# Projecting 27 instead of 28 features a head, feature by feature, beside a zero column in PSUM

## The chip, the cores and the metric

One NeuronCore of a Trainium2 chip runs the whole kernel. The metric is the device time of one execution in microseconds (us); a smaller number is better. The kernel before takes 399.32 us in the median of three runs (398.23 to 400.27).

## The reference, cut to what matters

Two linear attentions with a learned feature map (A and B, each with 16 heads of 28 features, on the same 2048 x 448 input x) are mixed by a gate per row. For each of the two:

```python
pq = einsum("bhsd,hdf->bhsf", q, w_phi)          # 28 features a head
pk = einsum("bhsd,hdf->bhsf", k, w_phi)
phi_q = concatenate([softmax(pq), softmax(-pq)])  # 56 features a head
phi_k = concatenate([softmax(pk), softmax(-pk)])
kv = einsum("bhsf,bhsd->bhfd", phi_k, v);  z = sum over s of phi_k
o = einsum("bhqf,bhfd->bhqd", phi_q, kv) / (einsum("bhqf,bhf->bhq", phi_q, z) + 1e-6)
y = o @ wo                                        # then g * y_A + (1 - g) * y_B
```

A softmax doesn't change when the same number is subtracted from all of its inputs. The two softmaxes of a head therefore need only the differences between its 28 projected features.

## The kernel before, in words

The rows of x are worked in 16 tiles of 128 (index t or k, i). Everything is float32, and products that need it are split into a high and a low part (`wkh`/`wkl`, `wqh`/`wql`, `wvh`/`wvl`, `xg`). The instructions are issued in the order in which the program is written, engine by engine; each engine works strictly in that order, and waits between engines come from which tile an instruction reads or writes. The order is therefore the schedule. In the profile PE is the matrix engine, PEld its weight loads, DVE, ACT and POOL the vector, scalar and GpSimd engines, SP the queue that issues all the DMAs.

**Start.** The projection weights of K are folded with `w_phi` on the chip: `bd` (L114) is a block-diagonal copy of `w_phi`, four heads in a block, and `fold` (L116 to L125) multiplies each 128-row part of the K weights by it: eight matmuls of 112 columns into a PSUM tile, a copy of the result to the high part on ACT (L124), the rest to the low part on DVE (L125). Ahead of the four folds 16 transposes of an identity run on PE into the same pool of PSUM tiles (`pw`, L244). In the trace each of these fp32 products is two PE records, so that 64 records stand for four folds.

**K and V phase** (loop at L264, 16 steps). A step of PE is the K projection (`proj`, L127 to L138: 11 matmuls for A, 11 for B, 448 columns each, into one PSUM tile of two banks), the V projection (the same with 450 and 448 columns) and `kv_acc` of the step before (L185, into the PSUM tile `one`). `shift` (L143) then reads the K tile four times on DVE: maximum (L147), minimum (L148), x minus the maximum (L151), the minimum minus x (L152), 896 elements a partition each; ACT takes exponentials (L154), DVE the sums (L161) and a reciprocal (L162), POOL multiplies (L165). The steps 2 to 5 also fold one part of the Q weights each. The pool `two` hands its three PSUM tiles of two banks out in turn to `pw`, the folds and all the projections.

**Q front.** `q_front` (L193) reads a Q projection from PSUM three times on DVE: a maximum over the features (L198, 896 elements) and the subtraction for A and for B (L200, 448 elements each), into `uq`. Four DMAs write that to DRAM (`qd`, L205) and one reads it back in another layout (`tq`, L206). Later `q_exp0`, `q_min`, `q_exp1` and `q_turn` (L212, L216, L217, L221, L229) take `tq` to the transposed features. The Q tiles 0 to 3 are projected in the last K and V steps (t = 13, 14) and right behind them (L316, L321), in that order with the turns of the tiles 0 and 1.

**Between the phases.** SP issues, behind the DMAs of the Q tiles, two large reads of the output weights (L325) and then the gate's small ones (`gates`, L253: L258 and L260); POOL and DVE need the gate for the first output tile (L261, L368 to L376).

**Output phase** (loop at L419). Step i: PE runs `num(i)` (L352), the Q projection i + 4 into its only PSUM tile `q` (L417), and the output matmul of tile i - 2 (L408). DVE runs, in this order, the transposition of `num` (`n_turn`, L358), a reciprocal (L367), the minimum of Q tile i + 2 (L216), two transpositions of o (L388, L389), a reciprocal (L374), `q_front(i + 4)` (L198, L200), L397 and `q_turn(i + 2)` (L229). The Q work ends with i = 11. In the last two tiles DVE also runs what POOL runs otherwise (L368 to L382); the gate is read there with a step of 16 elements (L375, `gate[:, None, :, :, i]`), and column DH of `ctrs` with a step of 32 (L368).

Of the kernel before, what the change touches and what calls it, by code (L numbers as in the profile page):

```python
# [8 lines left out]
F32 = mybir.dt.float32  # L9
F32R = mybir.dt.float32r  # L10
AF = mybir.ActivationFunctionType
OP = mybir.AluOpType
AX = mybir.AxisListType

P = 128
S, D, H, DH = 2048, 448, 16, 28
# [3 lines left out]
NP = H // 2  # L20
PF = 4 * DH
VC = 2 * D + 2
HP = 32
WARM = 16
LEAD = 4
# [5 lines left out]
def hedgehog_mix(ctx: ExitStack, tc: tile.TileContext, xd, wv, wkt, wqt, wphi, wo, cmask, cpmask, out):  # L31
    nc = tc.nc
# [3 lines left out]
    one_stack = ExitStack()  # L36
    one = one_stack.enter_context(tc.tile_pool(name="one", bufs=1, space=bass.MemoryType.PSUM))
    two_stack = ExitStack()
    two = two_stack.enter_context(tc.tile_pool(name="two", bufs=3, space=bass.MemoryType.PSUM))


    xg = [const.tile([P, 7, GT], F32R, name=f"xg{g}") for g in range(NG)]
# [1 line left out]
    gate = const.tile([P, 2, 4, NT], F32, name="gate")  # L44
    kvs = const.tile([P, 2, 2, 4, HP], F32, name="kvs")
    kvt = const.tile([P, 2, 2, 4, HP], F32, name="kvt")
    work = ctx.enter_context(tc.tile_pool(name="work", bufs=2))
# [7 lines left out]
    wp_ = ctx.enter_context(tc.tile_pool(name="wts", bufs=1))  # L55
# [5 lines left out]
    raw = start.enter_context(tc.tile_pool(name="raw", bufs=1, side="right"))  # L61
    ident = raw.tile([P, P], F32, name="ident")
    make_identity(nc, ident)
    mask = raw.tile([PF, 4], F32, name="mask")
    wp = raw.tile([PF, 2, 4, HP], F32, name="wp")
    bd = wp_.tile([PF, 2, 4, PF], F32, name="bd")
    wkh = wp_.tile([P, 4, 2 * D], F32R, name="wkh")
    wkl = wp_.tile([P, 4, 2 * D], F32R, name="wkl")
    wvh = wp_.tile([P, 4, VC], F32R, name="wvh")
    wvl = wp_.tile([P, 4, VC], F32R, name="wvl")  # L70
    NV = 2
# [24 lines left out]
    def load_wv(c):  # L96
        wvr[c] = raw.tile([P, VC], F32, name=f"wvr{c}")
        nc.sync.dma_start(wvr[c], wv[c * P:(c + 1) * P, :])
# [7 lines left out]
    wt = load_wt(wkt, 128)  # L106
# [3 lines left out]
    load_x(0, P, 2 * P, GT)  # L110
    for v in vs:
        nc.gpsimd.memset(v[:, :, :, :, DH:], 1.0)
    for q in range(4):
        nc.vector.tensor_scalar(bd[:, :, :, q * DH:(q + 1) * DH], wp[:, :, :, :DH], mask[:, q:q + 1], None, op0=OP.mult)  # L114

    def fold(c, wt, wh, wl):  # L116
        ps = two.tile([P, 2, 512], F32, name="two")
        for b in range(2):
            for g in range(4):
                nc.tensor.matmul(ps[:, b, g * PF:(g + 1) * PF], wt[:, b, g, c * P:(c + 1) * P], bd[:, b, g],  # L120
                                 start=True, stop=True)
        dh = wh[:, c, :].rearrange("p (b f) -> p b f", b=2)
        dl = wl[:, c, :].rearrange("p (b f) -> p b f", b=2)
        nc.scalar.activation(dh, ps[:, :, :D], AF.Copy)  # L124
        nc.vector.tensor_tensor(dl, ps[:, :, :D], dh.bitcast(F32), OP.subtract)  # L125

    def proj(t, wh, wl, widths, ps):  # L127
        x = xg[t // 4]
        o = (t % 4) * P
        lo = 0  # L130
        for b, n in enumerate(widths):
            terms = [(c, wh, c) for c in range(3)] + [(4 + c, wh, c) for c in range(3)]
            terms += [(3, wh, 3)] + [(c, wl, c) for c in range(4)]
            for i, (xc, w, wc) in enumerate(terms):
                nc.tensor.matmul(ps[:, b, :n], x[:, xc, o:o + P], w[:, wc, lo:lo + n],  # L135
                                 start=i == 0, stop=i == len(terms) - 1)
            lo += n
        return ps  # L138

    def hb(ap):  # L140
        return ap.rearrange("p b (h f) -> p b h f", f=DH)

    def shift(ps):  # L143
        p4 = hb(ps[:, :, :D])
        mx = ph.tile([P, 2, 2, H], F32, name="mx")
        e = ph.tile([P, 2, HA * DH], F32, name="e")
        nc.vector.tensor_reduce(mx[:, 0], p4, AX.X, OP.max)  # L147
        nc.vector.tensor_reduce(mx[:, 1], p4, AX.X, OP.min)  # L148
        e5 = e.rearrange("p s (b h f) -> p s b h f", b=2, f=DH)
        bc = [mx[:, s, :, :, None].to_broadcast([P, 2, H, DH]) for s in range(2)]  # L150
        nc.vector.tensor_tensor(e5[:, 0], p4, bc[0], OP.subtract)  # L151
        nc.vector.tensor_tensor(e5[:, 1], bc[1], p4, OP.subtract)  # L152
        for s in range(2):
            nc.scalar.activation(e[:, s], e[:, s], AF.Exp)  # L154
        return e
# [37 lines left out]
    def q_front(k, ps):  # L193
        seq[k] = len(seq) % 2
        u = uqs[k % len(uqs)]
        mx = work.tile([P, 2, H], F32, name="qmx")
        p4 = hb(ps[:, :, :D])
        nc.vector.tensor_reduce(mx, p4, AX.X, OP.max)  # L198
        for b in range(2):
            nc.vector.tensor_tensor(u[:, :, b], p4[:, b].rearrange("p (r g) f -> p r g f", r=4),  # L200
                                    mx[:, b].rearrange("p (r g) -> p r g", r=4)[:, :, :, None].to_broadcast([P, 4, 4, DH]),
                                    OP.subtract)
        m = qd[seq[k]]
        for c in range(4):
            nc.sync.dma_start(m[:, :, c].rearrange("r t x -> t r x"), u[32 * c:32 * c + 32].rearrange("p r b g f -> p r (b g f)"))  # L205
        nc.sync.dma_start(tq[seq[k]].rearrange("p c b g f -> p (c b g f)"), m.rearrange("r t c x -> (r t) (c x)"))  # L206
# [26 lines left out]
    def split_wo(c):  # L233
        n = 3 * D * (c % 2)
        st = [wtb[:, n + D * i:n + D * i + D] for i in range(3)]
        nc.sync.dma_start(st[0], wos[:, HP * c:HP * (c + 1), :])
        split_w(st[0], st[1].bitcast(F32R), st[2].bitcast(F32R), nc.gpsimd)
# [1 line left out]
            nc.sync.dma_start(wod[i][:, c], st[1 + i])  # L239


    pw = two.tile([P, 2, 512], F32, name="two")
    for i in range(WARM):
        nc.tensor.transpose(pw[:, 0, :P], ident, ident)  # L244
    for c in range(4):
        fold(c, wt, wkh, wkl)
        if c == 1:
            split_x(0, 0, P, nc.gpsimd)

    def two_tile():  # L250
        return two.tile([P, 2, 512], F32, name="two")

    def gates(lo, hi):  # L253
        gl = glog[:, lo:hi]
# [7 lines left out]

    phi = {}
    for t in range(NT):  # L264
        pk = proj(t, wkh, wkl, (D, D), two_tile())
        if t == 0:
            for c in range(4):
                split_w(wvr[c], wvh[:, c, :], wvl[:, c, :], nc.vector if c < 3 else nc.gpsimd)
            split_x(0, P, 2 * P, nc.gpsimd)
            split_x(0, 2 * P, GT, nc.gpsimd)  # L270
            load_x(1, 0, GT)
            wt = load_wt(wqt, 512)
            w5 = wos.rearrange("g (r b f) n -> b g r (f n)", r=4, b=2)
            for b in range(2):
                nc.sync.dma_start(w5[b], wo[b * D:(b + 1) * D, :].rearrange("(r g f) n -> g r (f n)", r=4, g=4))
        e = shift(pk)
        n = t - T0 - 1
        if 0 <= n < 2:
            q_exp0(n)
            q_min(n)  # L280
            q_exp1(n)
        phi[t] = k_soft(e)
        v_out(t, proj(t, wvh, wvl, (D + 2, D), two_tile()))
        if t in (1, 3, 5):
            g = (t + 1) // 2
            split_x(g, 0, GT, nc.gpsimd)
            if g + 1 < NG:
                load_x(g + 1, 0, GT)
        if t == 0:

            start.close()
            qp = ctx.enter_context(tc.tile_pool(name="qp", bufs=1, side="right"))
            wqh = qp.tile([P, 4, 2 * D], F32R, name="wqh")
            wql = qp.tile([P, 4, 2 * D], F32R, name="wql")
            uqs = [qp.tile([P, 4, 2, 4, DH], F32, name="uq")]
            tq = [qp.tile([P, 4, 2, 4, DH], F32, name=f"tq{i}") for i in range(2)]
        if 2 <= t < 6:
            fold(t - 2, wt, wqh, wql)
        if t == 6:
            eq = xrb.rearrange("p (s a c f) -> p s a c f", s=2, a=8, c=4)  # L300
            nc.gpsimd.memset(eq[:, :, :, :, DH:], 0.0)
            nc.gpsimd.memset(kvs, 0.0)
        if t > 0:
            kv_acc(t - 1, phi.pop(t - 1))
        if 6 <= t < 13:
            split_wo(t - 6)
        if t == NT - 4:
            gates(0, t + 1)
        if 0 <= n < 2:
            q_turn(n)  # L310
        n = t - T0
        if 0 <= n < 2:
            q_front(n, proj(n, wqh, wql, (D, D), two_tile()))


    q_front(2, proj(2, wqh, wql, (D, D), two_tile()))  # L316
    cb = [wp_.tile([P, 3592], F32, name=n) for n in ("wvh", "wvl")]
    ctrs = [c[:, :2048].rearrange("p (r b s c m) -> p r b s c m", r=4, b=2, s=2, m=HP) for c in cb]
    oTs = [c[:, 2048:2048 + (7 - MID) * P].rearrange("p (k t) -> p k t", t=P) for c in cb]
    uqs.append(cb[0][:, 2560:2560 + 2 * D].rearrange("p (r b g f) -> p r b g f", r=4, b=2, g=4))  # L320
    q_front(3, proj(3, wqh, wql, (D, D), two_tile()))  # L321
    woh = wp_.tile([P, 7, D], F32R, name="wkh")
    wol = wp_.tile([P, 7, D], F32R, name="wkl")
    for w, d in ((woh, wod[0]), (wol, wod[1])):
# [15 lines left out]
    qps = ctx.enter_context(tc.tile_pool(name="qps", bufs=1, space=bass.MemoryType.PSUM))  # L340
# [73 lines left out]
        nc.sync.dma_start(out[i * P:(i + 1) * P, :], ob)  # L414

    def q_proj(k):
        return proj(k, wqh, wql, (D, D), qps.tile([P, 2, 512], F32, name="q"))  # L417

    for i in range(NT + 2):  # L419
        f, m = i + LEAD, i + 2  # L420
        if i == 0:
            pq = q_proj(f)
        if i < NT:
            ps = num(i)
# [67 lines left out]
```

## Time and profile before

| | |
|---|---|
| median of three runs | 399.32 us (398.23 to 400.27) |
| span of the profiled execution, first to last instruction | 396.4 us |
| what lies around the span, against the median | 2.9 us |
| start (identity transposes, folds of K), to the first K matmul | 0 to 15 us |
| K and V phase | 15 to 161 us |
| Q tiles 0 to 3, with the last two K and V steps | 161 to 201 us |
| between the phases | 201 to 238 us |
| output phase with Q projections | 238 to 346 us |
| output phase without them | 346 to 396 us |

The profiled execution has no time of its own beside its span; the 2.9 us are the difference to the median. A row of a timeline reads: start, duration, engine, line, operation, output <- inputs, shape, and in brackets the idle time of the engine before it with what ended it. A row of the groups reads: count, total busy time, mean nanoseconds of one, idle time before.

### The profile page before, as it was taken

How to read it: one execution, taken by the hardware profiler on the slowest of the kernel's cores; microseconds unless marked ns; L12 is line 12 of the kernel's file. 1: busy time of each engine (PE TensorE's matmuls, PEld its weight loads, DVE VectorE, ACT ScalarE, POOL GpSimd, SP SyncE). 2: the span in 40 equal slices, each digit the busy share in tenths (PEclk: the TensorE clock that was granted, in tenths of full speed). 3: DMA queues.
4: the chain of work that ended last, by engine and by line, in shares of the span. 5: the costliest groups of instructions: out<-in, count | busy, mean ns of one | idle time of the engine just before them, and what ended most of it. 6: DMA issues, size and time to landing. Idle time of an engine off the chain costs nothing.

```text
span 396.4 us, 10423 instructions
## 1 busy us (share of the span) xinstructions
PE 360.8 (91%) x4608; PEld 320.3 (81%) x4608; DVE 294.0 (74%) x321; ACT 122.8 (31%) x174; POOL 220.6 (56%) x182
## 2 busy tenths in 40 slices
PE   8999999999999999999983089999999999997765
PEld 8999999999999999889872078988888888875544
DVE  1676767666666667669743299999999999988991
ACT  2744353233333333221400033333223333332112
POOL 0184816375444444304400299999888898889311
PEclk9999999999999999999997579999999999999989
DMA  7928411100222222131158133434443324420001
GB/s 179 311 65 268 182 48 56 53 25 25 88 68 67 67 67 70 28 95 46 48 132 319 64 94 94 117 119 118 117 119 115 102 69 120 116 96 26 25 23 46
DMA packets 27218, 38.52 MB, mean 97 GB/s; under 512 B 3733, under 2 KB 21893, under 8 KB 26885
## 3 DMA queue, kind: packets, MB, share of 16 engines
q1 hardware_dynamic: 27172, 37.85, 31.7%
q8 instruction: 36, 0.59, 0.6%
q14 instruction: 10, 0.07, 0.1%
HBM read 23.62 MB, written 15.84 MB: 100 GB/s over the span
## 4 chain that ended last, share of the span: by engine, by line
PE 71%; DMA 9%; DVE 9%; POOL 4%; SPq 3%; issue 2%; ACT 1%; POOLq 0%; DVEq 0%; ACTq 0%
PE two L135 33%; PE out L408 14%; PE q L135 12%; PE num L352 5%; PE two L120 4%; PE one L185 3%; DMA gd<-glog 3%; DMA qd<-uq 2%; DMA tq<-qd 2%; SPq L205 2%; POOL xrb L217 2%; DVE qmx L198 1%; DVE uq L200 1%; DVE wvh L358 1%; DMA wtb<-in_wkt 1%
## 5 line engine op out<-in xcount | busy, mean ns | idle before, releaser
L165 POOL TENSOR_TENSOR e<-e,rs 128x896 f32<-128x896 f32 x32 | 53.8, 1703 | 66.1 <-DVE rs L162 66.1
L408 PE MATMUL out<-wkh,e 128*128 128x448 f32 x224 | 52.8, 373 | 10.9 <-ACT bd L413 6.5
L154 ACT ACTIVATE e<-e 128x896 f32<-128x896 f32 x32 | 30.2, 954 | 98.7 <-DVE e L151 98.6
L135 PE MATMUL q<-wqh,xg 128*128 128x448 f32 x168 | 40.9, 384 | 17.3 <-DVE uq L200 14.5
L408 PEld LDWEIGHTS out<-wkh,e 128*128 128x128 f32 x224 | 41.5, 189 | 17.5 <-ACT bd L413 8.0
L135 PE MATMUL two<-wkh,xg 128*128 128x448 f32 x224 | 51.8, 369 | 0.0
L135 PE MATMUL two<-wvh,xg 128*128 128x450 f32 (+1 forms) x224 | 50.9, 366 | 0.0
L135 PEld LDWEIGHTS q<-wqh,xg 128*128 128x128 f32 x168 | 31.7, 194 | 22.6 <-DVE uq L200 14.9
L147 DVE TENSOR_REDUCE mx<-two 128x32 f32<-128x896 f32 x16 | 17.5, 1091 | 39.4 <-PE two L135 39.4
L135 PEld LDWEIGHTS two<-wvh,xg 128*128 128x128 f32 x224 | 42.1, 188 | 3.4
L135 PEld LDWEIGHTS two<-wkh,xg 128*128 128x128 f32 x224 | 40.9, 188 | 4.0 <-POOL xg L87 0.4
L217 POOL TENSOR_TENSOR xrb<-qmn,tq 128x896 f32<-128x896 f32 x16 | 28.2, 1762 | 23.7 <-DVE qmn L216 19.9
L229 DVE STREAM_TRANSPOSE wtb<-xrb 128x2048 f32<-128x2048 f32 x16 | 36.9, 2304 | 3.1 <-ACT xrb L221 3.1
L161 DVE TENSOR_REDUCE sm<-e 128x32 f32<-128x896 f32 x32 | 33.3, 1081 | 1.1
L352 PE MATMUL num<-wtb,kvt 32*32 32x128 f32 x2048 | 31.1, 283 | 2.4 <-DVE wvh L358 2.4
L352 PEld LDWEIGHTS num<-wtb,kvt 32*32 32x32 f32 x2048 | 25.0, 104 | 9.0 <-issue 3.4
L391 ACT ACTIVATE e<-turn 128x512 fp32r<-128x512 f32 x16 | 9.6, 598 | 70.7 <-DVE turn L388 70.7
L135 PE MATMUL two<-wvl,xg 128*128 128x450 f32 (+1 forms) x128 | 31.2, 365 | 0.0
L135 PE MATMUL two<-wkl,xg 128*128 128x448 f32 x128 | 30.9, 363 | 0.0
L408 PE MATMUL out<-wkl,e 128*128 128x448 f32 x112 | 26.8, 380 | 0.0
L135 PEld LDWEIGHTS two<-wvl,xg 128*128 128x128 f32 x128 | 24.1, 188 | 2.3 <-POOL wvl L102 0.3
L135 PEld LDWEIGHTS two<-wkl,xg 128*128 128x128 f32 x128 | 24.0, 187 | 1.8 <-DVE wkl L125 0.2
(92 smaller groups left out, 623.5 us busy)
## 6 DMA issues: line engine op xcount, KB each, us to landing
tq<-qd SPq DMA_DIRECT2D x16, 448.0 KB
qd<-uq SPq DMA_DIRECT2D x36, 112.0 KB
out<-bd SPq DMA_DIRECT2D x16, 224.0 KB
wod<-wtb SPq DMA_DIRECT2D x14, 224.0 KB
qd<-wvh SPq DMA_DIRECT2D x28, 112.0 KB
xrb<-in_xt SPq DMA_DIRECT2D x3, 1024.0 KB
wvr<-in_wv SPq DMA_DIRECT2D x4, 449.0 KB
wtb<-in_wkt SPq DMA_DIRECT2D x8, 224.0 KB
```

The costliest lines, as they stand in the source:

```text
L120: nc.tensor.matmul(ps[:, b, g * PF:(g + 1) * PF], wt[:, b, g, c * P:(c + 1) * P], bd[:, b, g], start=True, stop=True)
L135: nc.tensor.matmul(ps[:, b, :n], x[:, xc, o:o + P], w[:, wc, lo:lo + n], start=i == 0, stop=i == len(terms) - 1)
L147: nc.vector.tensor_reduce(mx[:, 0], p4, AX.X, OP.max)
L154: nc.scalar.activation(e[:, s], e[:, s], AF.Exp)
L161: nc.vector.tensor_reduce(sm[:, s], e[:, s].rearrange("p (h f) -> p h f", f=DH), AX.X, OP.add)
L165: nc.gpsimd.tensor_tensor(e3, e3, rs[:, s, :, None].to_broadcast([P, HA, DH]), OP.mult)
L185: nc.tensor.matmul(kvp[32 * r:32 * r + DH + 1, b, g], v[:, b, h // 2, h % 2], phi[:, :, hs:hs + DH], start=(t == 0 and b == 0 and g == 0), ...
L217: nc.gpsimd.tensor_tensor(eq[:, 1, :, :, :DH], mn.rearrange("p c a -> p a c")[:, :, :, None].to_broadcast([P, 8, 4, DH]), tview(k), OP.sub ...
L229: nc.vector.transpose(e_slot(k), eq.rearrange("p s a c f -> p (s a c f)"))
L352: nc.tensor.matmul(ps[32 * g:32 * g + 32, r, 2 * b + s], kvt[32 * r:32 * r + 32, b, s, g], eTs[i][32 * r:32 * r + 32, s, b, g], start=True ...
L391: nc.scalar.activation(hl[:, 0, :MID], ps, AF.Copy)
L408: nc.tensor.matmul(ps[:, :D], a, w, start=n == 0, stop=n == len(terms) - 1)
```

## The change

For each head the last column of `w_phi` is subtracted from the other 27 before the folding, so that the 28th feature is zero and isn't projected. `bd` has blocks of 27 columns; a fold's matmuls have 108 columns and its result is read with the features outermost, so that the folded weights are stored feature by feature (27 x 16 heads), 432 columns for A and for B. The K and Q projections write these 432 columns to columns 48 to 479 of a PSUM bank. The columns 480 to 495 are set to zero once, and nothing writes to them again; V keeps its columns 0 to 449. `shift` and `q_front` read columns 48 to 495 as 28 x 16, with the feature innermost: an element step of 16. For the zeros to last, the three PSUM tiles are allocated once and handed out by a counter, and the `q` tile of the output phase is allocated once as well.

```diff
+FD = DH - 1
+FW = H * FD
+FO, FZ = 48, 48 + H * FD
...
+    wpd = raw.tile([PF, 2, 4, FD], F32, name="wpd")
+    bd = wp_.tile([PF, 2, 4, 4 * FD], F32, name="bd")
...
+    nc.vector.tensor_tensor(wpd, wp[:, :, :, :FD], wp[:, :, :, FD:DH].to_broadcast([PF, 2, 4, FD]), OP.subtract)
     for q in range(4):
-        nc.vector.tensor_scalar(bd[:, :, :, q * DH:(q + 1) * DH], wp[:, :, :, :DH], mask[:, q:q + 1], None, op0=OP.mult)
+        nc.vector.tensor_scalar(bd[:, :, :, q * FD:(q + 1) * FD], wpd, mask[:, q:q + 1], None, op0=OP.mult)
+    twos = [two.tile([P, 2, 512], F32, name=f"two{i}") for i in range(3)]
...
+        return twos[turn_of[0] % 3]
...
+    for ps in twos:
+        nc.vector.memset(ps[:, :, FZ:FZ + H], 0.0)
...
     def fold(c, wt, wh, wl):
...
-        dh = wh[:, c, :].rearrange("p (b f) -> p b f", b=2)
-        nc.scalar.activation(dh, ps[:, :, :D], AF.Copy)
-        nc.vector.tensor_tensor(dl, ps[:, :, :D], dh.bitcast(F32), OP.subtract)
+        dh = wh[:, c, :].rearrange("p (b f h) -> p b f h", b=2, f=FD)
+        src = ps[:, :, :FW].rearrange("p b (h f) -> p b f h", f=FD)
+        nc.scalar.activation(dh, src, AF.Copy)
+        nc.vector.tensor_tensor(dl, src, dh.bitcast(F32), OP.subtract)
...
-                nc.tensor.matmul(ps[:, b, :n], x[:, xc, o:o + P], w[:, wc, lo:lo + n],
+                nc.tensor.matmul(ps[:, b, at:at + n], x[:, xc, o:o + P], w[:, wc, lo:lo + n],
...
+    def fm(ps):
+        return ps[:, :, FO:FO + D].rearrange("p b (f h) -> p b h f", h=H)
...
     def shift(ps):
-        p4 = hb(ps[:, :, :D])
+        p4 = fm(ps)
...
-    pw = two.tile([P, 2, 512], F32, name="two")
+    pw = two_tile()
...
-        pk = proj(t, wkh, wkl, (D, D), two_tile())
+        pk = proj(t, wkh, wkl, (FW, FW), two_tile(), FO)
...
     def q_proj(k):
-        return proj(k, wqh, wql, (D, D), qps.tile([P, 2, 512], F32, name="q"))
+        return proj(k, wqh, wql, (FW, FW), qt, FO)
+
+    qt = qps.tile([P, 2, 512], F32, name="q")
+    nc.vector.memset(qt[:, :, FZ:FZ + H], 0.0)
```

`q_front` changes as `shift` does, and the Q weights and the four Q projections outside the output phase as those of K.

More of the change, by code (lines that the diff above doesn't have):

```diff
@@ L38, in hedgehog_mix @@
     two_stack = ExitStack()
-    two = two_stack.enter_context(tc.tile_pool(name="two", bufs=3, space=bass.MemoryType.PSUM))
+    two = two_stack.enter_context(tc.tile_pool(name="two", bufs=1, space=bass.MemoryType.PSUM))
     xg = [const.tile([P, 7, GT], F32R, name=f"xg{g}") for g in range(NG)]
@@ L65, in hedgehog_mix @@
     wp = raw.tile([PF, 2, 4, HP], F32, name="wp")
-    bd = wp_.tile([PF, 2, 4, PF], F32, name="bd")
-    wkh = wp_.tile([P, 4, 2 * D], F32R, name="wkh")
-    wkl = wp_.tile([P, 4, 2 * D], F32R, name="wkl")
+    wpd = raw.tile([PF, 2, 4, FD], F32, name="wpd")
+    bd = wp_.tile([PF, 2, 4, 4 * FD], F32, name="bd")
+    wkh = wp_.tile([P, 4, 2 * FW], F32R, name="wkh")
+    wkl = wp_.tile([P, 4, 2 * FW], F32R, name="wkl")
     wvh = wp_.tile([P, 4, VC], F32R, name="wvh")
@@ L112, in hedgehog_mix, with two_tile, proj @@
         nc.gpsimd.memset(v[:, :, :, :, DH:], 1.0)
+    nc.vector.tensor_tensor(wpd, wp[:, :, :, :FD], wp[:, :, :, FD:DH].to_broadcast([PF, 2, 4, FD]), OP.subtract)
     for q in range(4):
-        nc.vector.tensor_scalar(bd[:, :, :, q * DH:(q + 1) * DH], wp[:, :, :, :DH], mask[:, q:q + 1], None, op0=OP.mult)
+        nc.vector.tensor_scalar(bd[:, :, :, q * FD:(q + 1) * FD], wpd, mask[:, q:q + 1], None, op0=OP.mult)
+    twos = [two.tile([P, 2, 512], F32, name=f"two{i}") for i in range(3)]
+    turn_of = [0]
+    def two_tile():
+        turn_of[0] += 1
+        return twos[turn_of[0] % 3]
+    for ps in twos:
+        nc.vector.memset(ps[:, :, FZ:FZ + H], 0.0)
     def fold(c, wt, wh, wl):
-        ps = two.tile([P, 2, 512], F32, name="two")
+        ps = two_tile()
         for b in range(2):
             for g in range(4):
-                nc.tensor.matmul(ps[:, b, g * PF:(g + 1) * PF], wt[:, b, g, c * P:(c + 1) * P], bd[:, b, g],
+                nc.tensor.matmul(ps[:, b, g * 4 * FD:(g + 1) * 4 * FD], wt[:, b, g, c * P:(c + 1) * P], bd[:, b, g],
                                  start=True, stop=True)
-        dh = wh[:, c, :].rearrange("p (b f) -> p b f", b=2)
-        dl = wl[:, c, :].rearrange("p (b f) -> p b f", b=2)
-        nc.scalar.activation(dh, ps[:, :, :D], AF.Copy)
-        nc.vector.tensor_tensor(dl, ps[:, :, :D], dh.bitcast(F32), OP.subtract)
-    def proj(t, wh, wl, widths, ps):
+        dh = wh[:, c, :].rearrange("p (b f h) -> p b f h", b=2, f=FD)
+        dl = wl[:, c, :].rearrange("p (b f h) -> p b f h", b=2, f=FD)
+        src = ps[:, :, :FW].rearrange("p b (h f) -> p b f h", f=FD)
+        nc.scalar.activation(dh, src, AF.Copy)
+        nc.vector.tensor_tensor(dl, src, dh.bitcast(F32), OP.subtract)
+    def proj(t, wh, wl, widths, ps, at=0):
         x = xg[t // 4]
@@ L196, in q_front @@
         mx = work.tile([P, 2, H], F32, name="qmx")
-        p4 = hb(ps[:, :, :D])
+        p4 = fm(ps)
         nc.vector.tensor_reduce(mx, p4, AX.X, OP.max)
@@ L248, in hedgehog_mix @@
             split_x(0, 0, P, nc.gpsimd)
-    def two_tile():
-        return two.tile([P, 2, 512], F32, name="two")
     def gates(lo, hi):
@@ L292, in hedgehog_mix @@
             qp = ctx.enter_context(tc.tile_pool(name="qp", bufs=1, side="right"))
-            wqh = qp.tile([P, 4, 2 * D], F32R, name="wqh")
-            wql = qp.tile([P, 4, 2 * D], F32R, name="wql")
+            wqh = qp.tile([P, 4, 2 * FW], F32R, name="wqh")
+            wql = qp.tile([P, 4, 2 * FW], F32R, name="wql")
             uqs = [qp.tile([P, 4, 2, 4, DH], F32, name="uq")]
@@ L312, in hedgehog_mix @@
         if 0 <= n < 2:
-            q_front(n, proj(n, wqh, wql, (D, D), two_tile()))
-    q_front(2, proj(2, wqh, wql, (D, D), two_tile()))
+            q_front(n, proj(n, wqh, wql, (FW, FW), two_tile(), FO))
+    q_front(2, proj(2, wqh, wql, (FW, FW), two_tile(), FO))
     cb = [wp_.tile([P, 3592], F32, name=n) for n in ("wvh", "wvl")]
@@ L320, in hedgehog_mix @@
     uqs.append(cb[0][:, 2560:2560 + 2 * D].rearrange("p (r b g f) -> p r b g f", r=4, b=2, g=4))
-    q_front(3, proj(3, wqh, wql, (D, D), two_tile()))
+    q_front(3, proj(3, wqh, wql, (FW, FW), two_tile(), FO))
     woh = wp_.tile([P, 7, D], F32R, name="wkh")
```

## The prediction

> **What bounds the kernel now.** I read the windows by stage first, since one average over the kernel would hide that its stages have different limits. Columns: stretch, its length, then busy time of PE, PEld, DVE, ACT and POOL with their instructions, granted clock, DMA share, GB/s.
>
> ```profile
> 92.00:161.00 69.00, 69.00 (x716) 62.20 (x718) 46.80 (x51) 22.23 (x36) 32.02 (x23) 1.00 0.21 68
> 161.00:201.00 40.00, 39.89 (x425) 35.88 (x412) 29.68 (x31) 10.61 (x16) 13.83 (x9) 1.00 0.19 49
> 201.00:238.00 37.00, 17.63 (x428) 14.84 (x428) 17.70 (x23) 5.46 (x9) 12.39 (x16) 0.72 0.50 162
> 238.00:346.00 108.00, 107.77 (x1652) 94.51 (x1654) 102.67 (x113) 34.50 (x50) 94.76 (x82) 1.00 0.40 110
> ```
>
> PE is never idle in the K and V phase, where DVE has a third to spare. Between the phases nobody is full. In the output phase PE is full again, and DVE nearly so. Next the chain of work that ended last, for what the time hangs on in each stage:
>
> ```profile
> 5.16 10.03 PE two L120 x64
> ...
> 141.67 9.09 PE two L135 x44
> 150.75 0.92 PE one L185 x64
> 151.68 9.09 PE two L135 x44
> ...
> 166.45 1.10 DVE qmx L198
> 167.57 1.17 DVE uq L200 x2
> ...
> 210.79 11.13 DMA gd<-glog
> ...
> 227.24 1.17 DVE uq L200 x2
> ...
> 249.14 4.71 PE q L135 x22
> ```
>
> PE carries it up to the first Q tile, in steps of 151.68 - 141.67 = 10.01 us. From 166 us on it goes through the Q front: DVE work, DMAs, the transposition, then the next Q tile on DVE; at 210.79 the gate's DMA, which SP issues behind the Q tiles, and after it the Q front of tile 4. From 238 us on it is PE. Last, DVE's timeline, for the slack that its readers have: once in the K phase, then its first and last transpositions of `num` in the output phase.
>
> ```profile
> 146.32 1.09 DVE L147 TENSOR_REDUCE mx<-two 128x32 f32<-128x896 f32 x1 [3.17 <-PE two L135]
> ```
>
> ```profile
> 230.83 2.27 DVE L358 STREAM_TRANSPOSE wvl<-num 128x2048 f32<-128x2048 f32 x1
> ...
> 240.82 2.27 DVE L358 STREAM_TRANSPOSE wvh<-num 128x2048 f32<-128x2048 f32 x1
> ...
> 347.04 2.32 DVE L358 STREAM_TRANSPOSE wvh<-num 128x2048 f32<-128x2048 f32 x1 [0.76 <-PE num L352]
> ```
>
> DVE idles 3.17 us of each K and V step. In the output phase its own step, back to back, is 240.82 - 230.83 = 9.99 us; the 11 steps to 347.04 take 116.21 us, 10.6 each, because PE slows the later ones and leaves DVE only 0.76 us a step.
>
> **The change part by part.**
>
> *Shorter projections, the gain.* A K and V step's 44 matmuls take 9.09 us, 206.6 ns each. In proportion 16 columns of 448 would be 7.4 ns. If the weight loads set the spacing it would be nothing: in the folds they seem to, as the next rows show (PE alone: the 16 transposes of 128 columns, and the folds' matmuls of 112 columns early and late).
>
> ```profile
> 1.30:5.10 3.80, 3.68 (x16) 3.28 (x16) 1.00 0.67 173
> ```
>
> ```profile
> 5.10:10.60 5.50, 5.44 (x25) 5.47 (x26) 1.00 1.12 231
> 10.70:15.00 4.30, 4.30 (x40) 4.30 (x39) 1.00 1.10 343
> ```
>
> 128 columns take 0.22 us and 112 columns the same 0.22 us, so that 108 instead of 112 in the folds is worth nothing. (Later the folds take 0.107 each; the granted clock reads 1.00 in both stretches, so it doesn't explain that.) From 112 columns at 107.5 ns to 448 at 206.6 the slope is 0.29 ns a column, 4.7 ns for 16. Between 4.7 and 7.4 I take 6 ns, and keep 0 as an end: 22 x 6 = 0.13 us a projection. On the path lie K0 to K13 and Q0, 15 x 0.13 = 1.95 us, and ten projections of the output phase, 1.3 us. K14, K15 and Q1 to Q3 lie beside the Q front's chain and bring nothing. In all 3.25 us, and only while PE stays the bound.
>
> *Strided reads on DVE, the cost.* Every reader of a projection now steps 16 elements, 64 bytes, from one element to the next. No row of before shows DVE reading PSUM that way. The nearest rows read SBUF: DVE's small products in the last tiles.
>
> ```profile
> L376 DVE TENSOR_TENSOR cdd<-crs,cden 128x64 f32<-128x64 f32 x2 | 0.5, 226 | 0.1
> L375 DVE TENSOR_TENSOR cden<-cden,gate 128x32 f32<-128x32 f32 x2 | 0.4, 214 | 0.1
> L369 DVE TENSOR_TENSOR cden<-cdd 128x32 f32<-128x32 f32 x2 | 0.4, 192 | 0.1
> L368 DVE TENSOR_TENSOR cdd<-wvl,crs 128x64 f32<-128x64 f32 x1 | 0.3, 261 | 0.0
> ```
>
> L375 reads the gate with the very step of 16. Against L369, 32 elements as well, it takes 22 ns more, 0.69 ns an element; L368, with a step of 32, takes 35 ns more than L376 for 64 elements, 0.55. Without stride an element costs (226 - 192) / 32 = 1.06. I bound the price in PSUM by 0 (a different memory) and 1.06 (an element costs two), and take 0.69, the row with the same step.
>
> [...]
>
> Per K step DVE gets 4 x 896 x 0.69 = 2.47 us more. The 3.17 us of idle time hide it, less the 0.13 that PE gives up: 0.57 left. That cover ends at (3.17 + 0.13) / 3584 = 0.92 ns an element. The K tile is held 2.5 us longer. Its next writer is V of the next step, which starts when that step's K is done, a step of 10.01 us after these readers began; four reads of 1.09 + 0.62 are over after 6.9, so this holds nothing up. Per Q tile it is 1792 x 0.69 = 1.24 us, and those lie on the path:
> - Q0, Q1, Q2 and Q4 stand in the chain one behind another (Q3's readers run beside SP's DMAs of Q2): 4 x 1.24 = 4.96 us.
> - In the output phase the step of DVE becomes 9.99 + 1.24 = 11.23, above PE's. Its 11 steps from tile 1 to tile 12 take 123.5 instead of 116.2: +7.3 us. PE's 1.3 us are then worth nothing, since PE waits.
>
> *Start.* The subtraction for `wpd` and four zeroings are added on DVE. The rows there (PE's transposes, DVE behind the mask, K0's waits for x and for the last fold's low part):
>
> ```profile
> 1.34 3.68 PE L244 MATMUL two<-ident 128*128 128x128 f32 x16 [1.34 <-POOL ident masks.py:199]
> ...
> 3.08 1.08 DVE L114 TENSOR_SCALAR bd<-wp,mask 112x224 f32<-112x224 f32 x4 [3.08 <-DMA mask<-in_cmask]
> 4.26 0.48 DVE L175 MEMSET one<- 128x512 f32 x1
> ...
> 15.82 0.71 PEld L135 LDWEIGHTS two<-wkh,xg 128*128 128x128 f32 x4 [0.38 <-POOL xg L87]
> ...
> 17.32 0.19 PEld L135 LDWEIGHTS two<-wkl,xg 128*128 128x128 f32 x1 [0.20 <-DVE wkl L125]
> ```
>
> The zeroing of a PSUM tile stands ahead of the transposes in the program, in the same bank though in other columns, and behind `wpd` and `bd` on DVE. If the transposes wait for it, they start at 3.08 + 0.38 (`wpd`, 216 elements at 1.06 on top of L369's 32) + 1.08 + 0.2 (two zeroings of 32 elements, by L369's 192 ns at most each, overlapping) = 4.75 instead of 1.34. Queued behind them on PE are all the folds, and behind these K0. 16 slots of 0.215 us, as in the rows above, end at 8.2, where the folds start now at 5.16, behind the landing of their weights: +3.05 us on the path. If no wait is set it is 0. If the quick spacing of the folds still sets in at 10.6 us, it is less, about 1.6. The trace can't say which; I take 3.05.
>
> [...]
>
> The last fold's copy (L124) and subtraction (L125) read 896 strided elements each, one after the other: 2 x 896 x 0.69 = 1.24 us. K0 waits for L125 at 17.32 already, so that this is on the path. If ACT reads strides freely, half of it goes. The other zeroing, of the `q` tile, stands behind the gate's small DVE work, and the first Q projection of the output phase waits for it; what that costs ends in the time in which DVE stands still for the gate:
>
> ```profile
> 225.91 0.35 DVE L374 RECIPROCAL cden<-cden 128x32 f32<-128x32 f32 x1 [13.00 <-POOL cden L369]
> ```
>
> That is 13 us of cover.
>
> *Sum.* 3.05 + 1.24 - 1.95 + 4.96 + 7.3 = +14.6 us: a span of 411.0 instead of 396.4, and with the 2.9 us between span and median **413.9 us**.
>
> **The rivals.**
>
> *A: strides in PSUM are free, the transposes wait.* 3.05 less the 0.38 us that K0 now waits for x anyway, - 1.95 - 1.3 = -0.6: **398.7 us**. For it: PSUM isn't SBUF, and the strided rows above are all SBUF.
>
> *B: strides free and no wait, the other side.* -3.25: **396.1 us**, faster. The mechanism is PE's shorter matmul in the two stages where PE is full. It decides where a strided element costs less than 3.25 us / (1792 in the last fold + 4 x 1792 in the Q front) = 0.36 ns more, and in the output phase below (0.76 + 0.13) / 1.792 = 0.50. Against it: L375 and L368 lie above both.
>
> *C: an element costs two, 1.06 more.* The K step's readers need 3.8 us, over the 3.3 there are: DVE's step is 10.01 - 3.17 + 3.8 = 10.64, with a fold's 896 elements at 2.12 it is 12.5, and DVE replaces PE as the bound of the K phase. K0's readers start 5 us late (3.05 and 2 x 896 x 1.06); nine steps and four with a fold bring K13's some 15 us late; K14's and K15's readers then push the Q front's chain, four times 1.9 us come on top, tile 1 of the output phase is some 25 us late, and 11 steps of 11.9 add 14.6: **439 us**. Against it: no row of DVE shows such a price.
>
> *D: the matmuls don't get shorter,* because the loads set their spacing. That takes 3.25 from the gains of A and B (402, 399.3), 1.95 from the forecast's. Against it: the spacing of the 448 is far above the folds' 0.107, whose weights have as many columns. I count it within the others' margins.
>
> **How the numbers follow.** Forecast 0.42, A 0.30, B 0.10, C (or dearer) 0.18. The forecast's own range is 408 (price 0.55, start 1.6) to 420 (price up to 0.9, where the K phase would join). The range of 395.5 to 422 takes in the forecast, A and B, and leaves C out. This kernel's measurement can tell some 0.5% from no change, 2 us. Faster by more: B's 0.10, and 0.08 of A's 0.30 (a wait shorter than 3.05); within: 0.20 of A; slower: 0.42 + 0.18, and 0.02 of A, 0.62.
>
> **What would show it.** L147 to L152 and L198 at about 1.08 + 0.62 = 1.7 us instead of 1.08, and L200 at 0.93 instead of 0.62, would confirm the price; at 1.08, A or B holds; at 2.0, C. The first identity transpose near 4.7 us shows the wait. In the K phase PE must still be back to back, a step about 0.13 us shorter. In the output phase L358 must start every 11.2 us without waiting for `num`, and PE must wait for L200. I am wrong most of all if PSUM serves single elements as fast as runs, for then 13.5 of the 14.6 us go.

## The result and the profile after

The changed kernel takes 394.54 us in the median of six runs (393.09 to 395.19), the kernel before 398.42 us (398.06 to 400.27) beside it. The ratio is 0.9884, with a 95% interval of 0.9863 to 0.9904: 1.2% faster, 3.9 us, where 413.9 us were forecast, 14.6 us more than before. The profiled execution of the changed kernel took 395.19 us, with a span of 393.4.

I begin with the disputed rows, DVE's readers of the projections. These are the groups of the changed kernel on DVE, different shapes kept apart (count, busy time, mean ns of one, idle time before):

```profile
L165 DVE TENSOR_REDUCE mx<-two 128x32 f32<-128x896 f32 x16 | 17.5, 1091 | 38.2 <-PE two L150 38.2
L169 DVE TENSOR_TENSOR e<-two,mx 128x896 f32<-128x896 f32 x16 | 17.3, 1081 | 0.0
...
L216 DVE TENSOR_REDUCE qmx<-q 128x32 f32<-128x896 f32 x12 | 12.3, 1029 | 0.0
...
L218 DVE TENSOR_TENSOR uq<-q,qmx 128x448 f32<-128x448 f32 x12 | 6.9, 620 | 0.2
...
L140 DVE TENSOR_TENSOR wkl<-two,wkh 128x864 fp32r<-128x864 f32 x4 | 4.2, 1058 | 7.9 <-ACT wkh L139 7.9
```

The same groups of the kernel before:

```profile
L147 DVE TENSOR_REDUCE mx<-two 128x32 f32<-128x896 f32 x16 | 17.5, 1091 | 39.4 <-PE two L135 39.4
L151 DVE TENSOR_TENSOR e<-two,mx 128x896 f32<-128x896 f32 x16 | 17.3, 1081 | 0.0
...
L198 DVE TENSOR_REDUCE qmx<-q 128x32 f32<-128x896 f32 x12 | 12.3, 1027 | 0.0
...
L200 DVE TENSOR_TENSOR uq<-q,qmx 128x448 f32<-128x448 f32 x12 | 6.9, 619 | 0.2
```

A step of 16 elements in PSUM costs DVE nothing: 1091 against 1091 ns, 1081 against 1081, 1029 against 1027, 620 against 619. The subtraction of a fold (L140), which now steps 27 elements, takes 1058 ns for 864 elements and took 1092 for 896.

Next the start. The timeline of the changed kernel (start, duration, engine, line, in brackets the idle time before):

```profile
4.25 0.16 DVE L128 MEMSET two<- 128x32 f32 x3
...
4.51 3.37 PE L262 MATMUL two<-ident 128*128 128x128 f32 x16 [4.51 <-DVE two L128]
...
7.72 7.29 PE L134 MATMUL two<-bd,wtb 112*128 112x108 f32 x64
...
14.79 1.74 PE L150 MATMUL two<-wkh,xg 128*128 128x432 f32 x7
...
15.48 0.70 PEld L150 LDWEIGHTS two<-wkh,xg 128*128 128x128 f32 x4 [0.23 <-POOL xg L91]
```

The wait is there, as forecast: the transposes start at 4.51 us (4.75 was estimated, 1.34 was before), released by the zeroing L128. The folds start at 7.72 instead of 5.16. But they now take 7.29 us instead of 10.03, with 64 records both times, and the first K matmul comes at 14.79; the kernel before has it at

```profile
14.96 1.94 PE L135 MATMUL two<-wkh,xg 128*128 128x448 f32 x7
```

so that the forecast's +3.05 us is -0.17 here. K0's fourth product then waits for POOL's part of x, at 15.48 us; in the kernel before it did so at 15.82.

Now the chain of work that ended last, of the changed kernel (start, us, what), in the places that the prediction showed of before:

```profile
140.41 8.99 PE two L150 x44
...
150.32 9.01 PE two L150 x44
...
164.83 1.10 DVE qmx L216
...
208.19 11.61 DMA gd<-glog
...
236.13 6.15 PE q L150 x22
...
248.37 4.54 PE q L150 x22
252.91 4.26 PE out L423 x21
...
259.00 4.54 PE q L150 x22
```

A K step is 150.32 - 140.41 = 9.91 us (10.01 before), and Q0's maximum comes at 164.83 instead of 166.45, 1.62 us earlier. A step of the output phase is 259.00 - 248.37 = 10.63 us. Before, the same chain reads

```profile
249.14 4.71 PE q L135 x22
253.86 4.33 PE out L408 x21
...
260.02 4.71 PE q L135 x22
```

10.88 us; the Q projection gives 0.17 of the difference and, although nothing about it was changed, the output matmul 0.07. The first Q projection of the phase takes 6.15 us instead of 4.54. The windows of the changed kernel show why (stretch, length, PE busy with its instructions, granted clock, DMA share, GB/s):

```profile
236.00:240.00 4.00, 3.87 (x12) 0.57 0.46 115
240.00:246.00 6.00, 6.00 (x32) 1.00 0.22 76
```

The granted clock is 0.57 there and 1.00 behind it. The change doesn't force that: in another execution of the same kernel (e11 below) the same projection takes 4.60 us. Last, DVE's transpositions of `num` in the output phase of the changed kernel:

```profile
228.82 2.27 DVE L373 STREAM_TRANSPOSE wvl<-num 128x2048 f32<-128x2048 f32 x1
...
238.81 2.27 DVE L373 STREAM_TRANSPOSE wvh<-num 128x2048 f32<-128x2048 f32 x1
...
344.10 2.32 DVE L373 STREAM_TRANSPOSE wvh<-num 128x2048 f32<-128x2048 f32 x1 [0.52 <-PE num L367]
```

DVE's own step is 238.81 - 228.82 = 9.99 us as before, and it still waits for PE, 0.52 us a step instead of 0.76. PE is still the bound of this phase.

Where the 3.0 us of the two spans (396.4 - 393.4) went: 1.62 up to Q0's maximum; 0.39 more up to tile 1's transposition (228.82 against 230.83), a stretch in which the gate's DMA takes 11.61 instead of 11.13 us; 116.21 - 115.28 = 0.93 in the 11 steps, of which the low clock has taken some 1.6 back (6.15 - 4.54); behind these nothing (49.3 against 49.4).

### The profile page after: what moved, and what is told of

The parts are those of the page before. It is cut to its first block, busy times and chain, and to the rows that moved or that the text cites. A ratio compares the mean times of both kernels' runs of the same rounds, so it can differ in the third digit from the quotient of the medians.

```text
span 393.4 us, 10387 instructions
## 1 busy us (share of the span) xinstructions
PE 355.6 (90%) x4608; PEld 320.0 (81%) x4608; DVE 294.4 (75%) x326; ACT 122.8 (31%) x174; POOL 220.7 (56%) x182
## 4 chain that ended last, share of the span: by engine, by line
PE 71%; DVE 10%; DMA 8%; POOL 4%; issue 2%; SPq 2%; ACT 2%; POOLq 0%; DVEq 0%; ACTq 0%
PE two L150 33%; PE out L423 14%; PE q L150 12%; PE num L367 5%; PE two L134 4%; PE one L203 3%; DMA gd<-glog 3%; POOL xrb L235 2%; DMA tq<-qd 2%; DMA qd<-uq 2%; DVE wtb L247 1%; SPq L223 1%; DVE wvh L373 1%; DVE wvl L373 1%; DVE qmx L216 1%
## 5 line engine op out<-in xcount | busy, mean ns | idle before, releaser
L150 PE MATMUL q<-wqh,xg 128*128 128x432 f32 x168 | 41.6, 391 | 13.9 <-DVE uq L218 8.9
L150 PE MATMUL two<-wkh,xg 128*128 128x432 f32 x224 | 50.7, 365 | 0.0
L150 PEld LDWEIGHTS q<-wqh,xg 128*128 128x128 f32 x168 | 33.3, 204 | 18.2 <-DVE uq L218 9.4
L165 DVE TENSOR_REDUCE mx<-two 128x32 f32<-128x896 f32 x16 | 17.5, 1091 | 38.2 <-PE two L150 38.2
L150 PE MATMUL two<-wkl,xg 128*128 128x432 f32 x128 | 30.6, 360 | 0.0
L373 DVE STREAM_TRANSPOSE wvh<-num 128x2048 f32<-128x2048 f32 x8 | 18.4, 2306 | 10.4 <-PE num L367 10.4
```

The costliest lines, as they stand in the source:

```text
L150: nc.tensor.matmul(ps[:, b, at:at + n], x[:, xc, o:o + P], w[:, wc, lo:lo + n], start=i == 0, stop=i == len(terms) - 1)
L373: nc.vector.transpose(cb[i % 2][:, :2048], ps.rearrange("p r a t -> p (r a t)"))
```

## The experiments

The theory after the result: strided reads in PSUM are free, the wait of the transposes is covered, and PE's shorter matmuls are the whole gain. Rivals: the strided reads do cost, and something else pays for them; or the zeroing and the fixed tiles bring or take something; or the wait costs what was forecast and hides a larger gain.

**e1: the strided reads alone**, in the kernel before.

```diff
+    def fm(ps):
+        return ps[:, :, :D].rearrange("p b (f h) -> p b h f", h=H)
...
     def shift(ps):
-        p4 = hb(ps[:, :, :D])
+        p4 = fm(ps)
...
-        p4 = hb(ps[:, :, :D])
+        p4 = fm(ps)
         nc.vector.tensor_reduce(mx, p4, AX.X, OP.max)
```

> The kernel before, in which the K and Q readers on DVE take the 448 projected columns of PSUM with a step of 16 elements (so features of different heads are mixed in one softmax; nothing else changes). Theory: a strided element of PSUM costs DVE nothing more, so the maximum over 896 elements stays at 1.09 us, the subtraction of 448 at 0.62, and the time at 398.4 us, within 0.3%. Rival, the price of the prediction (0.69 ns an element): 1.7 and 0.93 us, and about 410.5 us (12 us more: 5 in the Q front, 7.3 in the output phase). Rival, strides free in the changed kernel only because 16 columns lie in a row across heads: not told apart by this run, since the step is the same.

Measured: 399.43 us, ratio 1.0004 [0.9989, 1.0020] to the kernel before. Its groups on DVE:

```profile
L150 DVE TENSOR_REDUCE mx<-two 128x32 f32<-128x896 f32 x16 | 17.5, 1092 | 39.7 <-PE two L135 39.7
...
L201 DVE TENSOR_REDUCE qmx<-q 128x32 f32<-128x896 f32 x12 | 12.3, 1028 | 0.0
...
L203 DVE TENSOR_TENSOR uq<-q,qmx 128x448 f32<-128x448 f32 x12 | 6.9, 620 | 0.2
```

The strided reads are free by themselves, row by row and in the whole time. The first rival falls.

**e2: the shorter matmuls alone.** In each K and Q projection the first of 11 products keeps its 448 columns, the other ten have 432.

```diff
+                m = n - cut if i else n
-                nc.tensor.matmul(ps[:, b, :n], x[:, xc, o:o + P], w[:, wc, lo:lo + n],
+                nc.tensor.matmul(ps[:, b, :m], x[:, xc, o:o + P], w[:, wc, lo:lo + m],
```

> The kernel before, in which 10 of the 11 matmuls of each K and Q product run over 432 instead of 448 columns (the last 16 columns get only the first product; no stride, no new tiles, no zeroing, same start). Theory: all of the gain is PE's shorter matmuls, so that 10/11 of it comes: a K step 9.92 us instead of 10.01, an output step 10.65 instead of 10.87, 394.9 us (-3.5). Rival: part of the gain is the start or the tiles that are allocated once; then this run stays over 396.5 us.

Measured: 395.23 us, ratio 0.9905 [0.9881, 0.9929]. The gain is 0.95%; 11/10 of that is 1.05%, and the whole change gives 1.16%, within the intervals. The chain of e2's profile has the changed kernel's steps as well:

```profile
141.01 9.00 PE two L136 x44
...
150.93 8.98 PE two L136 x44
...
247.47 4.58 PE q L136 x22
...
258.14 4.57 PE q L136 x22
```

A K step is 9.92 us and an output step 10.67, where 9.92 and 10.65 were expected. So PE's shorter matmuls account for the gain.

**e3: the zeroing and the fixed tiles alone**, in the kernel before (the zeroed columns are its unused 480 to 495).

```diff
+    twos = [two.tile([P, 2, 512], F32, name=f"two{i}") for i in range(3)]
...
+    for ps in twos:
+        nc.vector.memset(ps[:, :, 480:480 + H], 0.0)
...
-        ps = two.tile([P, 2, 512], F32, name="two")
+        ps = two_tile()
```

> The kernel before with its three PSUM tiles allocated once and columns 480 to 495 of each set to zero ahead of the identity transposes; 28 features as before. Theory: the transposes wait for the zeroing (first one near 4.4 us instead of 1.34, folds near 7.6 instead of 5.16), but the first K matmul still comes near 15 us, since the folds then run at the quick spacing from the start: 398.4 us, within 0.4%. Rival, the prediction's term: +3.05, 401.5 us. Rival, the fixed tiles bring part of the gain: below 397 us.

Measured: 399.15 us, ratio 1.0003 [0.9989, 1.0017]. PE's timeline of this kernel:

```profile
4.41 3.37 PE L254 MATMUL two<-ident 128*128 128x128 f32 x16 [4.41 <-DVE two L124]
7.62 7.35 PE L130 MATMUL two<-bd,wtb 112*128 112x112 f32 x64
15.32 1.28 PE L145 MATMUL two<-wkh,xg 128*128 128x448 f32 x3 [0.34 <-ACT xg L85]
```

The wait is the changed kernel's wait (4.41 us), and the time is that of before: the interval leaves it at most 0.17%, 0.7 us, of the 3.05. What covers it is seen in e1, whose transposes don't wait; this is PE's timeline of e1:

```profile
1.34 3.33 PE L247 MATMUL two<-ident 128*128 128x128 f32 x16 [1.34 <-POOL ident masks.py:199]
4.96 2.01 PE L120 MATMUL two<-bd,wtb 112*128 112x112 f32 x16 [0.29 <-DMA wtb<-in_wkt]
8.26 4.24 PE L120 MATMUL two<-bd,wtb 112*128 112x112 f32 x32 [1.28 <-DMA wtb<-in_wkt]
12.81 2.21 PE L120 MATMUL two<-bd,wtb 112*128 112x112 f32 x16 [0.31 <-DMA wtb<-in_wkt]
15.19 1.28 PE L135 MATMUL two<-wkh,xg 128*128 128x448 f32 x3 [0.17 <-ACT xg L85]
```

Here the folds run at the quick spacing from their first one (2.01 / 16 = 0.126 us), start 2.7 us before those of e3, and wait for the chunks of the K weights instead (0.29, 1.28, 0.31 us). Their first K matmul comes at 15.19, that of e3 at 15.32. Starting the folds earlier buys a wait for DMAs. Behind the folds stands one more: ACT's copy of x waits for the DMA of x (0.88 us before, 0.74 in the changed kernel, 1.48 in e8, 2.61 in e9), and K0's fourth product waits for POOL's part of x, between 15.30 and 17.00 us, wherever the folds start (15.82 before, 15.48 in the changed kernel, 16.88 in e1, 16.48 in e2, 17.00 in e3, 15.30 in e9).

**e4: the transposes ahead of the zeroing**, in the changed kernel: the zeroing now waits for the transposes.

```diff
+    pw = two_tile()
+    for i in range(WARM):
+        nc.tensor.transpose(pw[:, 0, :P], ident, ident)
     for ps in twos:
         nc.vector.memset(ps[:, :, FZ:FZ + H], 0.0)
```

> The changed kernel with the identity transposes ahead of the zeroing in the program, so that PE doesn't wait and the zeroing waits for PE instead. Theory: transposes at 1.34, folds near 5.2 us; when the first K matmul comes depends on when the clock of PE goes up (10.7 us in the trace of before, 7.6 in that of the changed kernel), so it lies between 13.4 and 15, and the time between 393 and 394.5 us. Rival, the wait is a plain cost: 2.5 us less than the changed kernel, 392 us, in every execution.

Measured: 393.37 us, 0.9890 [0.9844, 0.9936]. That is no difference from the changed kernel, but the spread wasn't expected: four executions took 392.70 to 393.49 us, two took 398.0, and one of the two is the profiled one. PE's timeline in it:

```profile
1.34 3.68 PE L129 MATMUL two<-ident 128*128 128x128 f32 x16 [1.34 <-POOL ident masks.py:199]
5.28 13.99 PE L137 MATMUL two<-bd,wtb 112*128 112x108 f32 x64 [0.27 <-DVE two L131]
18.96 2.23 PE L153 MATMUL two<-wkh,xg 128*128 128x432 f32 x7
```

and the window over that stretch (PE busy with its instructions, granted clock, DMA share, GB/s):

```profile
1.34:18.96 17.62, 17.35 (x81) 1.00 1.00 266
```

All 64 records of the folds run at 13.99 / 64 = 0.219 us, the slow spacing, and the first K matmul is 4.2 us later than in the changed kernel's profile (18.96 against 14.79). That is most of the 4.9 us between the two groups; that the four shorter executions start like the changed kernel's is inferred, since none of them was profiled.

The clock column reads 1.00 over all of that stretch. The traces of the two kernels hold the clock as a list of records, and the first one, of 1.00, lies at 10.74 us in the kernel before and at 7.47 in the changed kernel; the column counts all that lies ahead of it as 1.00. In both traces the spacing changes at that record, among the folds of the one and the transposes of the other, from 213 ns between two starts to 112. No record gives the clock ahead of it; that the slow spacing is a lower clock is my reading, which no run here shows. What the start costs thus goes with the time at which the quick spacing begins, and that varies between executions: e1 and the kernel before issue the same start, but e1's first 16 fold records stand 0.126 us apart, from 4.96 us on, while those of the kernel before stay at 0.213 up to 10.6 us.

**e5: the same strides in SBUF**, in the kernel before: the sums of the exponentials step 16 elements.

```diff
-            nc.vector.tensor_reduce(sm[:, s], e[:, s].rearrange("p (h f) -> p h f", f=DH), AX.X, OP.add)
+            nc.vector.tensor_reduce(sm[:, s].rearrange("p (b h) -> p b h", b=2),
+                                    e[:, s].rearrange("p (b f h) -> p b h f", b=2, h=H), AX.X, OP.add)
```

> The kernel before, in which the sums of the exponentials (DVE, 896 elements from SBUF, twice a K step) read with a step of 16 elements, so that they sum over elements of different heads; PSUM is read as before. Theory: SBUF charges for single elements what the gate's row showed (0.69 ns), so one sum takes 1.08 + 0.62 = 1.70 us, while PSUM charges nothing; the 1.24 us a step are hidden by DVE's idle 3.17, and the time stays at 399.2 us, within 0.4%. Rival: the gate's row and its neighbour differ for another reason, and SBUF charges nothing either: 1.08 us a sum.

Measured: 400.16 us, ratio 1.0036 [1.0017, 1.0054]. Its group and a piece of DVE's timeline:

```profile
L161 DVE TENSOR_REDUCE sm<-e 128x32 f32<-128x896 f32 x32 | 53.7, 1718 | 1.1
```

```profile
146.55 1.09 DVE L147 TENSOR_REDUCE mx<-two 128x32 f32<-128x896 f32 x1 [1.92 <-PE two L135]
```

The kernel before takes 1081 ns for this line. (1718 - 1081) / 896 = 0.71 ns an element: the prediction's price of 0.69 holds in SBUF, for a reduction of the same size and step as the one for which PSUM asks 0. The idle time of a K step falls from 3.17 to 1.92 us and hides the extra of that phase. The whole is 0.36% slower; less than 0.4% was expected, and the interval allows more. In the profiles the two kernels part in the Q front: Q0's maximum comes at 166.68 us against 166.45, the gate's DMA starts at 212.89 against 210.79, and tile 1's transposition comes at 232.7 instead of 230.8 us.

**e6: matmuls of 336 columns** in ten of 11 products, the edit of e2 with a cut of 112 instead of 16.

```diff
-        pk = proj(t, wkh, wkl, (D, D), two_tile())
+        pk = proj(t, wkh, wkl, (D, D), two_tile(), 7 * H)
```

> The kernel before with 10 of the 11 matmuls of each K and Q product over 336 instead of 448 columns (the last 112 columns get only the first product). What a column costs: in proportion 0.46 ns, so that the spacing falls by 52 ns and a K step of 10.01 us by 1.03; by the 4.5 ns that 16 columns saved in a K step, 0.28 ns, by 0.63; by the 7.7 ns of the output phase, 0.48 ns, by 1.08. If the weight loads set the spacing it stops falling somewhere above 188 ns, and the step loses less than 0.3.

Measured in one execution, so without an interval: 379.94 us, span 378.2. The chain and DVE's timeline:

```profile
140.52 8.14 PE two L136 x44
...
149.59 3.72 PE two L136 x22
```

```profile
239.11 2.27 DVE L359 STREAM_TRANSPOSE wvl<-num 128x2048 f32<-128x2048 f32 x1
...
249.10 2.28 DVE L359 STREAM_TRANSPOSE wvh<-num 128x2048 f32<-128x2048 f32 x1
```

A K step is 9.07 us, 0.94 less than before; 20 shortened products give 47 ns each, 0.42 ns a column. The spacing still follows the columns at 336, so the weight loads don't set it at 432 (rival D). In the output phase DVE starts a tile every 249.10 - 239.11 = 9.99 us without waiting for PE: here lies the floor that the change came close to (10.63).

**e8 and e11: the changed kernel again**, on two more occasions, and **e9 and e10: the zeroings as DVE's first instructions**, ahead of the subtraction for `wpd` and of `bd`.

```diff
+    twos = [two.tile([P, 2, 512], F32, name=f"two{i}") for i in range(3)]
+    for ps in twos:
+        nc.vector.memset(ps[:, :, FZ:FZ + H], 0.0)
...
     def load_x(g, *cuts):
...
-    for ps in twos:
-        nc.vector.memset(ps[:, :, FZ:FZ + H], 0.0)
```

> The changed kernel once more, on the chip of the other runs: 0.988 of the kernel before, and no execution several us above the others. If its start hangs on when the clock of PE goes up, its executions fall into two groups, as those with the transposes ahead of the zeroing did (393 and 398 us).

> The changed kernel with the three zeroings as DVE's first instructions, ahead of the DMA that the subtraction of the last column waits for, so that neither the transposes nor the folds wait for them: transposes near 1.4 us, folds near 5.2. Theory: the start is bounded by the DMAs of the weights and of x (first K matmul near 15 us whatever the folds' start), so the time is that of the changed kernel, within 0.3%. Rival: the wait costs its 2.5 us, and this version takes 0.982 of the kernel before.

> The changed kernel with the zeroings as DVE's first instructions once more, beside the changed kernel on the same chip, with more rounds. Theory (the transposes' wait for the zeroing lies behind the start's DMAs and costs nothing): same ratio as the changed kernel within 0.2%, 0.987 to 0.990. Rival (the wait costs 1 us or more that the spread has hidden so far): 0.25% or more below the changed kernel, with intervals that don't overlap.

> The changed kernel as it is, as the other half of that comparison: 0.987 to 0.991 by both.

| | us, median | ratio to the kernel before | first K matmul in the profile |
|---|---|---|---|
| e8, changed | 393.58 (392.96 to 397.43) | 0.9891 [0.9856, 0.9926] | 15.03 |
| e9, zeroing first | 394.00 (392.13 to 395.32) | 0.9870 [0.9848, 0.9892] | 13.61 |
| e10, zeroing first | 394.35 (392.57 to 394.44) | 0.9867 [0.9846, 0.9889] | 14.12 |
| e11, changed | 394.11 (393.45 to 395.71) | 0.9885 [0.9862, 0.9909] | 15.29 |

PE's timeline of e9:

```profile
1.34 3.67 PE L262 MATMUL two<-ident 128*128 128x128 f32 x16 [1.34 <-POOL ident masks.py:199]
...
13.61 1.25 PE L150 MATMUL two<-wkh,xg 128*128 128x432 f32 x3 [0.16 <-ACT xg L92]
15.30 1.06 PE L150 MATMUL two<-wkh,xg 128*128 128x432 f32 x4 [0.44 <-POOL xg L94]
```

The transposes start at 1.34 again. In their profiles the first K matmul comes 0.7 to 1.7 us earlier, but the fourth waits for x (15.30), and no gain shows in the medians; the ratios lie 0.2% apart with intervals that overlap. The rival's 0.982, a saving of 2.5 us, lies outside both intervals; a saving of up to some 1.8 us isn't excluded (the two differences, -0.0021 and -0.0018, taken together with their intervals). So no version was found that beats the changed kernel by more than the measurement can tell. e8's expectation that no execution would lie several us above the others failed: one took 397.43 us, 3.9 above the median. That one wasn't profiled, so that a late start as in e4 can only be supposed.

e11's chain also answers for the output phase without the low clock (its windows read 1.00 from 236 to 246 us):

```profile
235.93 4.60 PE q L150 x22
```

The 11 steps from tile 1 to tile 12 take 113.73 us in e11 (342.35 - 228.62), against 115.28 in the changed kernel's first profile and 116.21 before.

## Why the prediction was wrong

- **"Strided reads on DVE, the cost": the step that failed.** It carried 0.69 ns an element from rows that read SBUF to reads of PSUM. In PSUM the price is 0 (e1, and the rows after); in SBUF it is 0.71 (e5). With it go 1.24 us in the last fold, 4.96 in the Q front and 7.3 in the output phase, 13.5 of the 14.6 us. The prediction had 0 as the other end and named this as what would make it wrong; it chose the row nearest in step over the difference in memory.
- **The wait of the transposes: there, but not on the path.** Its place and its size were right (4.51, estimated 4.75). The sum took 3.05 us for it by keeping the slots of 0.215 us up to 8.2 and the folds as slow behind them as before; in the changed kernel's three profiles the folds start at 7.7 to 8.0 us, and their 64 records take 7.29 us, 7.29 (e8) and 7.52 (e11) instead of 10.03. e3 gives the wait 0.0% [-0.1, +0.2]. Without the wait the folds run into the K weights' DMAs (e1, up to 1.28 us) or the K matmuls into x (e9, 0.44 us). The prediction's sentence that the clock reads 1.00 in both stretches and so doesn't explain the two spacings read a column without a record: the first clock record of the kernel before lies at 10.74 us, where its spacing changes. That a wait is set at all was my choice between two values, since no row of before shows one; no run shows the 3.05 us. The traces of the changed kernel (4.51 us) and of e3 (4.41) show the wait; whether it is set for the bank or for the tile no run here tells apart.
- **The gain: right in its place, a little off in its terms.** A K step gives 0.10 us instead of 0.13 (4.5 ns a shortened matmul instead of 6), a Q projection of the output phase 0.17 instead of 0.13 (7.7 ns). Together with the output matmul's 0.07 that makes 0.24 a step, some 2.5 us in ten steps, where the prediction counted "worth nothing, since PE waits": that followed from the strided price, and fell with it. Right was that 108 columns instead of 112 bring the folds nothing: e3's 64 records of 112 columns take 7.35 us, the changed kernel's 64 of 108 take 7.29.
- **Which rival it was.** B's time (396.1) lies nearest and its mechanism, PE's shorter matmul where PE is full, is the one that e2 shows. In one point A was right instead: the wait does exist. B was held unlikely because L375 and L368 lay above its threshold of 0.36 ns; these rows were of the other memory. Its number has some luck in it: B has no wait at all, and the wait that is there costs nothing because x and the K weights come late.
- **A small term: what lies around the span.** The sum adds 2.9 us to the span. All executions of the record with both numbers take 1.7 to 1.9 us more than their span, so that the profiled one was quicker than the median and the sum some 1.1 us too high by this.
- **What stays open**: why 16 columns are worth more in a Q projection than in a K projection. It lies in the kernel before: from its first start to the next group's, its Q projection takes 4.62 us (249.07 to 253.69 in PE's timeline) and its K projection 4.52 (151.61 to 156.13), both with 448 columns, while the changed kernel's take 4.45 both (248.30 to 252.75, 150.25 to 154.70). Why the unchanged output matmuls run 0.07 us quicker beside it: they do so in e2 as well (4.26 us at 252.05), without the stride and the zeroing, so that it comes with the shorter matmuls. And what makes the quick spacing at the start begin at one time or another (7.47 us in the changed kernel, 10.74 before).

## What to carry to other kernels

The step of 16 elements cost DVE 0.71 ns an element in SBUF (e5) and nothing in PSUM (e1): before a price is carried from one memory to the other, test the pattern by itself; one kernel such as e1 decides it. The wait at the start was counted at 3.05 us and cost nothing (e3, 0.0%), for the K weights and x came late as well: look for the DMAs behind a wait before counting it in full. The clock column read 1.00 at a spacing of 213 ns as at 112, since the trace has no record ahead of 10.74 us (before): look at the spacing of equal instructions there. Where PE is full in a phase, count every column taken from it, up to the step of the next engine (here DVE's 9.99 us).

## What was not expected of the hardware

- DVE reads PSUM with a step of 16 elements (64 bytes) at the rate of a contiguous read, 1091 ns for 896 elements, while the same step in SBUF takes 1718 instead of 1081 ns. ACT's copy of a fold reads PSUM in the new order, with a step of 27 elements, without a notable loss as well: 887 ns for 864 elements, 913 for 896.
- The records of PE's fp32 products at the start stand 213 ns apart ahead of the trace's first clock record and 112 ns behind it, in the traces of both kernels. That record lies 2.96 us behind the first transpose in the changed kernel (4.51 and 7.47) and 9.40 us in the kernel before (1.34 and 10.74). In e4 the slow spacing holds for all transposes and folds: PE works from 1.34 to 18.96 us, 17.35 of 17.62 us busy, and the folds' records stand 0.219 us apart. What sets the time of the change no run here shows.
- A stretch of low granted clock follows the time between the phases in the changed kernel's first profile (0.57 between 236 and 240 us) and in e10 (0.63), where e8, e9 and e11 read 1.00. The first Q projection of the output phase takes 6.15 and 6.13 us in the two, and 4.60, 4.61 and 4.60 in the three others: 1.55 us more in the changed kernel's (6.15 against 4.60).
